# Two-product sums left in PSUM, raw words loaded earlier, and early row sums spread over query tiles, in a three-layer kernel

## The chip, the cores and the metric

The kernel runs on one core of one Trainium2 chip. The metric is the device time of one execution in microseconds (us). The notation of the profile: PE is TensorE, PEld its weight loads, DVE is VectorE, ACT is ScalarE, POOL is GpSimd and SP is the engine that issues most DMAs.

## The reference, cut to what matters

```python
# attention with keys and values averaged over groups of 8 positions
k_p = k.reshape(B, H, Sp, 8, D).mean(axis=3); v_p = v.reshape(B, H, Sp, 8, D).mean(axis=3)
scores = scale * q @ k_p.T ; attn = softmax(scores) ; x = attn @ v_p        # B=4, H=8, S=576, D=64
# layer 1: mixture of experts, all experts on all tokens, N=2304, D=512, E=8, F=1024
P = exp(x @ w_gate - max); eight times: P /= rows' sums, P /= columns' sums, P *= N / E
out = sum over e of P[:, e] * (maximum(x @ w1[e], 0) @ w2[e])
# layer 2: gated, F2=1536, its weights given as 64-bit floats
g = out @ w_gate2; silu = g / (1 + exp(-g)); result = (silu * (out @ w_val)) @ w_out
```

All arithmetic is to be accurate to fp32. Each fp32 operand of a matmul is split into a rounded half and a low part, and a product takes three matmuls (half times half, half times low part, low part times half).

## The kernel before

**Tiling.** The 2304 tokens are worked in three passes of TB = 768, each as two halves of HB = 384. The matrices of the experts are cut into 30 "quads" (a quad is 256 columns of w1 and the 256 rows of w2 that go with them; the first half of expert 0 is done apart, in the attention phase). Each quad's first product is a 2x2 block product done with seven products M1 to M7 in place of eight. Operands are the blocks B11, B21, B22 and the differences T1 to T4 of the token matrix. Each product is six matmuls of 128x384. Four results come out of them: "11" = M1 + M2, "21" (M1 + M6 + M7 + M4, all accumulated in one PSUM bank), "22" and "12". Three of the four are two-product sums: a bank of PSUM plus a partial sum that ScalarE had copied to SBUF (`part_sum`, line 1016: s1, u2, u3).

**PSUM.** Bank `a` has two buffers and holds the running sum M1, M6, M7, M4. Bank `b` has one and holds M2. Bank `c` holds M5, then M3 on top of it; it has two buffers in pass 0 and in the gated layer, one in passes 1 and 2.

**Stages.** (1) Attention, with the first half of expert 0 as filler for TensorE (`ready`, `fill`, `group0_units`); the loop runs over 20 query tiles. At the end of each tile, early_row_sums does four steps of the row sums of w2's blocks on GpSimd (line 187), their rounding on ScalarE (line 204), their low part on GpSimd (line 208), a store; these are later operands of the second product. (2) Pass 0, `quad`: seven products, then the second product tile by tile (`second_tile`, matmuls of 128x512 at lines 1086 to 1088), its result scaled by the routing weight and added in SBUF by VectorE (line 1328). From quad NEARLY on, row sums are made in this pass on VectorE (`row_sums`, line 187). (3) Passes 1 and 2, `expert_quad`, quads in pairs (q = 0, 1): the seven products of the first layer, weighting by the routing weight before the second product, and that one again in seven-product form (`block`, 12 matmuls of 128x384, accumulated into AC by VectorE at line 1270). The pairs number 30; the blocks of a pair are placed among the products of the next. A pair is 168 matmuls. (4) A tail of seven blocks, then the gated layer, 18 times a gate quad and a value quad (`gate_sink`, `value_sink`).

**Order.** All engines run the instructions in the order in which the program writes them; nothing is rescheduled. `late` is a queue of instructions that are issued at the next point between products (`later`). `side` is a queue of small steps, one of which is taken ("popped") at each point between products and after each block: 10 pops in the first quad of a pair, 11 in the second. The routing's iterations go through it in pass 0, the conversion of the gated layer's 64-bit weights in passes 1 and 2. For the conversion (`conv64`, `conv_steps`), a half block of raw words is loaded into one of two buffers of 512 KB, ScalarE takes the magnitude (line 934), VectorE does four more operations on 128x512 words and a fifth (line 951) that frees the buffer, GpSimd adds the two parts. Two halves make a block, 36 halves in all. All of these loads, as those of the experts' sets, go through the one SP queue, which waits in order.

**Around the weighting in passes 1 and 2.** `csum` writes a two-product sum to SBUF (line 1382), `weigh` takes the maximum with 0 times the routing weight (line 1390), in SBUF except for "21"; "22" and "12" are weighted in one 128x768 operation. `split_h` makes the rounded half on ScalarE (line 1227) and the low part on VectorE or GpSimd (line 1228); `sum_t13` and `sum_t24` (lines 1235, 1239) make the differences for the second product on GpSimd. The points at which they are issued are listed by hand with `on(q, point, ...)`, where a point is a product's name or the number of a block of the pair.

**Routing weights.** `load_pb` loads the weights of one expert and one pass, the same row for all 128 partitions; in the buffer in HBM a row lies in pieces of 128 floats.

## Time and profile before

| what | value |
|---|---|
| runs of the kernel | 2148.04, 2145.79, 2142.83 us; median 2145.79 |
| profiled execution | 2147.0 us; span of the core 2145.3 |
| TensorE busy | 2020.7 us, 94% of the span |
| VectorE, ScalarE, GpSimd busy | 1599.8 (75%), 806.2 (38%), 1323.7 (62%) |
[...]
| attention | to about 276 us |
| pass 0 | 276.5 to 766.9 us |
| passes 1 and 2 | 766.9 to 1716.9 us |
| gated layer | 1716.9 to 2145.3 us |

The stages are told by the first matmul on B11 of each quad. Matmuls overlap in the pipeline, so the busy time of TensorE hides short waits; the time per matmul in a stretch tells more. [...]

### The profile page before, as it was taken

The numbers are of one execution on the slowest core, as the hardware profiler recorded it, in microseconds if no ns is written. First come the engines' busy times: TensorE is split into PE (matmuls) and PEld (weight loads), VectorE is DVE, ScalarE is ACT, GpSimd is POOL, SyncE is SP. The second block draws the span as 40 slices with busy tenths as digits, with TensorE's granted clock in tenths as the row PEclk, the third lists the DMA queues.
The fourth block names the chain that finished last, engine by engine and source line by source line (L and its number), as shares of the span: only waits on it lengthen the run. The fifth ranks groups of instructions, "written<-read, shape, count | busy, mean of one in ns | idle before, by whom it ended". The sixth has DMA issues, their size and how long they took to land.

```text
span 2145.3 us, 30456 instructions
## 1 busy us (share of the span) xinstructions
PE 2020.7 (94%) x11079; PEld 1903.8 (89%) x11079; DVE 1599.8 (75%) x2119; ACT 806.2 (38%) x1461; POOL 1323.7 (62%) x1005
## 2 busy tenths in 40 slices
PE   7778789999999999999999999999999989999999
PEld 6677778888888889999999989998999889899898
DVE  7554366778778778997888888987655767767776
ACT  3333333444444442232322332332232354544543
POOL 4544556678788835767777656776655556445442
PEclk9989999999999999999999999999999999999999
DMA  6455457678888888888988888888888655453442
GB/s 175 138 150 142 123 201 253 224 281 298 289 284 304 291 276 310 307 293 306 310 299 315 276 285 310 298 315 300 267 261 258 211 191 166 168 193 131 163 140 96
DMA packets 227925, 514.82 MB, mean 240 GB/s; under 512 B 35424, under 2 KB 120000, under 8 KB 221632
## 3 DMA queue, kind: packets, MB, share of 16 engines
q1 hardware_dynamic: 222880, 497.15, 68.0%
q0 software_dynamic: 4896, 15.73, 2.6%
q8 instruction: 88, 1.44, 0.3%
q14 instruction: 61, 0.50, 0.1%
HBM read 361.78 MB, written 151.04 MB: 239 GB/s over the span
## 4 chain that ended last, share of the span: by engine, by line
PE 52%; DVE 22%; DMA 10%; issue 6%; POOL 5%; ACT 3%; SPq 1%; POOLq 0%; ACTq 0%; DVEq 0%
PE aps L114 5%; PE aps L116 5%; PE aps L115 5%; PE yps L1086 4%; PE yps L1088 4%; PE yps L1087 4%; PE mbs L114 4%; PE mbs L115 3%; PE mbs L116 3%; PE cps L114 3%; PE cps L116 2%; PE cps L115 2%; DVE LF L1390 2%; DVE LF L187 2%; DVE AC L1270 2%
## 5 line engine op out<-in xcount | busy, mean ns | idle before, releaser
L1016 ACT COPY LF<-aps 128x384 f32<-128x384 f32 x378 | 179.6, 475 | 536.8 <-PE aps L116 536.7
L114 PE MATMUL mbs<-LR 128*128 128x384 f32 x840 | 288.1, 343 | 10.0 <-DVE AC L1270 5.1
L115 PE MATMUL mbs<-LR 128*128 128x384 f32 x840 | 285.8, 340 | 1.0 <-DVE LR L1228 1.0
L116 PE MATMUL mbs<-LR 128*128 128x384 f32 x840 | 284.7, 339 | 0.0
L1228 POOL TENSOR_TENSOR LR<-LF,LR 128x768 fp32r<-128x768 f32 (+1 forms) x148 | 243.5, 1666 | 60.1 <-ACT LR L1227 56.7
L1227 ACT ACTIVATE LR<-LF 128x768 fp32r<-128x768 f32 (+1 forms) x240 | 174.7, 761 | 208.1 <-DVE LF L1390 180.1
L1270 DVE TENSOR_TENSOR AC<-mbs,AC 128x768 f32<-128x768 f32 x196 | 185.9, 950 | 75.4 <-PE mbs L116 74.8
L1086 PE MATMUL yps<-LR 128*128 128x512 f32 x576 | 228.5, 397 | 12.1 <-DVE AC L1328 11.7
L1088 PE MATMUL yps<-LR 128*128 128x512 f32 x576 | 225.6, 392 | 0.5 <-DVE LR L1532 0.5
L1087 PE MATMUL yps<-LR 128*128 128x512 f32 x576 | 225.4, 391 | 0.0
L770 POOL TENSOR_TENSOR LR<-praw,LR 128x512 fp32r<-128x512 f32 (+1 forms) x130 | 135.2, 1060 | 140.9 <-ACT LR L764 140.9
L1239 POOL TENSOR_TENSOR LF<-LF 128x384 f32<-128x384 f32 x120 | 154.1, 1284 | 95.3 <-DVE LR L1228 90.6
L770 POOL TENSOR_TENSOR LR<-sums,LR 128x1024 fp32r<-128x1024 f32 x65 | 160.0, 2462 | 53.5 <-ACT LR L764 53.4
L1235 POOL TENSOR_TENSOR LF<-LF 128x768 f32<-128x768 f32 x60 | 117.2, 1954 | 122.5 <-DVE LF L1390 122.4
L114 PEld LDWEIGHTS mbs<-LR 128*128 128x128 f32 x840 | 160.3, 191 | 14.3 <-DVE AC L1270 8.9
L115 PEld LDWEIGHTS mbs<-LR 128*128 128x128 f32 x840 | 160.6, 191 | 1.3 <-DVE LR L1228 1.3
L116 PEld LDWEIGHTS mbs<-LR 128*128 128x128 f32 x840 | 160.2, 191 | 0.0
L66 POOL TENSOR_TENSOR LR<-rraw,LR 128x512 fp32r<-128x512 f32 x72 | 112.9, 1590 | 68.6 <-ACT LR L65 58.1
L1086 PEld LDWEIGHTS yps<-LR 128*128 128x128 f32 x576 | 108.5, 188 | 37.8 <-DVE AC L1328 18.6
L1390 DVE SCALAR_TENSOR_TENSOR LF<-LF,LR 128x384 f32<-128x384 f32 x120 | 138.4, 1154 | 4.1
L1328 DVE SCALAR_TENSOR_TENSOR AC<-yps,pr,AC 128x512 f32<-128x512 f32 x168 | 121.0, 742 | 25.3 <-PE yps L1088 25.2
L1088 PEld LDWEIGHTS yps<-LR 128*128 128x128 f32 x576 | 108.5, 188 | 24.5 <-DVE LR L1532 1.0
(289 smaller groups left out, 5750.1 us busy)
## 6 DMA issues: line engine op xcount, KB each, us to landing
LR<-w1s_d SPq DMA_DIRECT2D x210, 512.0 KB, 5.8
LR<-w2s_d SPq DMA_DIRECT2D x210, 512.0 KB, 5.6
w1s_d<-LR SPq DMA_DIRECT2D x29, 1792.0 KB, 8.5
w2s_d<-LR SPq DMA_DIRECT2D x90, 256.0 KB, 5.7
w2s_d<-LR SPq DMA_DIRECT2D x22, 1024.0 KB, 4.2
praw<-in_moe_w_dram SPq DMA_DIRECT2D x30, 512.0 KB, 5.2
rraw<-in_moe_w_dram SPq DMA_DIRECT2D x30, 512.0 KB, 4.5
LR<-rows_d POOLq DMA_DIRECT2D x12, 1024.0 KB, 7.1
```

The source lines that it names most:

```text
L114: nc.tensor.matmul(ps, lhsT=wh, rhs=ah, start=start, stop=False, skip_group_check=more)
L115: nc.tensor.matmul(ps, lhsT=wh, rhs=al, start=False, stop=False, skip_group_check=more)
L116: nc.tensor.matmul(ps, lhsT=wl, rhs=ah, start=False, stop=stop, skip_group_check=more)
L770: nc.gpsimd.tensor_tensor(out=lo, in0=src, in1=hi.bitcast(F32), op=ALU.subtract)
L1016: nc.scalar.copy(out=t, in_=ps[:, :HB])
L1086: nc.tensor.matmul(ps, lhsT=hh[:, o:o + P], rhs=wh, start=j == 0, stop=False)
L1087: nc.tensor.matmul(ps, lhsT=hh[:, o:o + P], rhs=wl, start=False, stop=False)
L1088: nc.tensor.matmul(ps, lhsT=hl[:, o:o + P], rhs=wh, start=False, stop=j == 1)
L1227: nc.scalar.activation(out=hi, in_=src, func=AF.Copy)
L1228: f = lambda: eng.tensor_tensor(out=lo, in0=src, in1=hi.bitcast(F32), op=ALU.subtract)
L1270: nc.vector.tensor_tensor(out=acc_of(m), in0=ps[:, :, :HB], in1=acc_of(m), op=ALU.add)
L1390: nc.vector.scalar_tensor_tensor(out=r, in0=r if src is None else src[:, :HB], scalar=0.0, in1=w, op0=ALU.max, op1=ALU.mult)
```

## The change

- Early row sums: 7 instead of 8. One step per query tile instead of four: the four sums in one tile; in the next the rounding, the low parts and the next load; the store one tile later still.
- Routing weights are laid out in HBM so that one expert's row of a pass is contiguous (768 floats); the one store becomes 12.
- Conversion: the load of a half stands 7 pops ahead of its first use (before 4) and two pops behind the fifth step (before one); a half takes 14 pops (before 11), the stores stand later.
- `whole`: a two-product sum is written back into its bank of PSUM; "22", whose bank `c` is needed for M3, goes to a new buffer of bank `b`. All users read it from there: in pass 0 and the gated layer ScalarE and VectorE, in passes 1 and 2 the weighting, which for "11", "22" and "21" writes to PSUM again.
- `split_b`, for "11", "22" and "21": ScalarE copies the weighted value to SBUF (for GpSimd's differences) and rounds it, VectorE takes the low part from PSUM. "12" goes to SBUF only. `split_t`, for the differences, has both low parts on GpSimd.
- The points of `split_b`, `split_t` and the differences move.
- The transposed result of pass 0 (`transposed`) goes to the free half of AC instead of a two-deep buffer.

```diff
-    P_d = dram.tile([NT - TT, E, P], F32, name="P_d")
+    P_d = dram.tile([E, N - TB], F32, name="P_d")
-    NEARLY = 8
+    NEARLY = 7
...
-        for i in range(NEARLY):
+        def load(i):
             r = rawp.tile([P, 2, DM], F32, tag="raw", name=f"early{i}")
             nc.sync.dma_start(out=r, in_=rows[i].rearrange("(j p) d -> p j d", p=P))
+            return r
+
+        r = load(0)
+        for i in range(NEARLY):
             yield
+            if i > 0:
+                keep_row_sums(i - 1, w)
             for f in take_row_sums(nc.gpsimd, r, t):
                 f()
-                yield
+            yield
             nc.scalar.activation(out=w[:, :, 0], in_=t, func=AF.Copy)
-            yield
             for c in range(2):
...
-                yield
-            keep_row_sums(i, w)
+            if i + 1 < NEARLY:
+                r = load(i + 1)
+        yield
+        keep_row_sums(NEARLY - 1, w)
...
-                for _ in range(4):
-                    next(early_sums, None)
+                next(early_sums, None)
...
-            side.append(lambda: nc.sync.dma_start(out=P_d.rearrange("t e c -> (t e) c"), in_=pt[:n, 0:P]))
+            def store():
+                for t in range(NT - TT):
+                    nc.sync.dma_start(out=P_d[:, t * P:(t + 1) * P], in_=pt[t * E:(t + 1) * E, 0:P])
+            side.append(store)
...
-            yield from [loads[0], n, n, n]
-            stored = n
+            yield from [loads[0]] + [n] * 6
             for i, (halves, begin, out_sums, store) in enumerate(pairs):
                 for j, (_, c) in enumerate(halves):
-                    yield from [c[0], stored, c[1], c[2], begin if j == 0 else n, c[3], c[4], loads[2 * i + j + 1],
-                                n, out_sums if j == 1 else n, n]
-                    stored = store if j == 1 else n
-            yield from [n, stored]
+                    yield from [c[0], c[1], c[2], n if j else begin, c[3], c[4], n, loads[2 * i + j + 1],
+                                out_sums if j else n, n, n, n, store if j else n, n]
...
+        def whole(name, ps, t):
+            if t is None:
+                return ps[:, :HB]
+            out = (new_b() if name == "22" else ps)[:, :HB]
+            nc.vector.tensor_tensor(out=out, in0=ps[:, :HB], in1=t, op=ALU.add)
+            return out
...
-                src = ps[:, :HB]
-                if t is not None:
-                    src = part_of(TEMP[name], HB, F32)
-                    nc.vector.tensor_tensor(out=src, in0=ps[:, :HB], in1=t, op=ALU.add)
+                src = whole(name, ps, t)
...
-            x2 = part_of(16.5 + 2 * (t % 2), DM, F32).rearrange("p (k t) -> p k t", k=KD)
+            x2 = acc_view(TT + t).rearrange("p (k t) -> p k t", k=KD)
...
-                src = P_d[(p - 1) * TT:p * TT, e, :]
-                nc.sync.dma_start(out=pb_of(p * E + e).rearrange("p (t c) -> p t c", t=TT),
-                                  in_=src.partition_broadcast(P))
+                nc.sync.dma_start(out=pb_of(p * E + e), in_=P_d[e, (p - 1) * TB:p * TB].partition_broadcast(P))
...
+        def split_b(q, m, name):
+            src = weighed.pop((q, name))
+            hi, lo = h_of(q, m)
+            nc.scalar.copy(out=r_of(q, name), in_=src)
+            nc.scalar.activation(out=hi, in_=src, func=AF.Copy)
+            late.append(lambda: nc.vector.tensor_tensor(out=lo, in0=src, in1=hi.bitcast(F32), op=ALU.subtract))
...
+        def split_t(q, m, name, eng):
+            hi, lo = (h_pair(q, m, 2)[:, :, h] for h in (0, 1))
+            src = r_of(q, name, 2)
             nc.scalar.activation(out=hi, in_=src, func=AF.Copy)
             f = lambda: eng.tensor_tensor(out=lo, in0=src, in1=hi.bitcast(F32), op=ALU.subtract)
...
-            def csum(name, ps, t):
-                nc.vector.tensor_tensor(out=r_of(q, name), in0=ps[:, :HB], in1=t, op=ALU.add)
-
-            def weigh(name, n, src=None):
-                r = r_of(q, name, n)
+            def weigh(name, ps, t):
+                src = whole(name, ps, t)
                 h = int(name[1]) - 1
-                w = pb[:, h * HB:(h + 1) * HB]
-                if n > 1:
-                    w = w.unsqueeze(1).to_broadcast([P, n, HB])
-                nc.vector.scalar_tensor_tensor(out=r, in0=r if src is None else src[:, :HB], scalar=0.0, in1=w,
+                if name == "12":
+                    out = r_of(q, name)
+                else:
+                    out = weighed[q, name] = src
+                nc.vector.scalar_tensor_tensor(out=out, in0=src, scalar=0.0, in1=pb[:, h * HB:(h + 1) * HB],
                                                op0=ALU.max, op1=ALU.mult)
...
-            point("M2", lambda: csum("11", banks["b"], s1), lambda: weigh("11", 1))
+            point("M2", lambda: weigh("11", banks["b"], s1))
...
-            point("M7", lambda: csum("22", banks["c"], u3))
+            point("M7", lambda: weigh("22", banks["c"], u3))
...
-            point("M4", lambda: weigh("21", 1, banks["a"]))
+            point("M4", lambda: weigh("21", banks["a"], None))
...
-            point("M3", lambda: csum("12", banks["c"], u2), lambda: weigh("12", 2))
+            point("M3", lambda: weigh("12", banks["c"], u2))
...
-            on(0, 1, lambda: split_h(0, "M1", "11", 1, G))
-            on(0, "M3", lambda: sum_t13(0))
-            on(1, 3, lambda: split_h(0, "M3", "22", 2, V))
-            on(1, "M6", lambda: sum_t24(0))
-            on(1, 4, lambda: split_h(0, "M5", "11", 2, G), lambda: split_h(1, "M1", "11", 1, G))
-            on(1, "M3", lambda: sum_t13(1))
-            on(1, 6, lambda: split_h(1, "M3", "22", 2, V), lambda: split_h(0, "M6", "22", 2, V))
+            on(0, 0, lambda: split_b(0, "M1", "11"))
+            on(0, 2, lambda: split_b(0, "M3", "22"))
+            on(0, "M3", lambda: split_b(0, "M2", "21"))
+            on(1, "M1", lambda: sum_t13(0), lambda: sum_t24(0))
+            on(1, 3, lambda: split_b(1, "M1", "11"))
+            on(1, 4, lambda: split_t(0, "M5", "11", G))
+            on(1, 5, lambda: split_b(1, "M3", "22"))
+            on(1, "M3", lambda: split_b(1, "M2", "21"))
+            on(1, 6, lambda: split_t(0, "M6", "22", G), lambda: sum_t13(1), lambda: sum_t24(1))
...
-            on(0, "M2", lambda: sum_t24(1))
-            on(0, 1, lambda last=last: split_h(1, "M5", "11", 2, V if last else G))
-            on(0, 2, lambda last=last: split_h(1, "M6", "22", 2, V if last else G))
+            on(0, 1, lambda last=last: split_t(1, "M5", "11", V if last else G))
+            on(0, 2, lambda last=last: split_t(1, "M6", "22", V if last else G))
...
-                nc.vector.tensor_tensor(out=g, in0=src, in1=g, op=ALU.mult)
+                src = whole(name, ps, t)
+                nc.vector.tensor_tensor(out=src, in0=src, in1=g, op=ALU.mult)
```

## Rows read from the trace of the kernel before

**Rows 1.** Busy time of each engine in seven stretches (columns as in the second line).
```profile
core 0: us, PE busy (x) PEld busy (x) DVE busy (x) ACT busy (x) POOL busy (x), PEclk, DMA share, GB/s
85.00:241.00 156.00, 118.97 (x801) 109.00 (x800) 64.77 (x113) 50.86 (x101) 74.25 (x88) 0.88 0.60 161
375.70:406.70 31.00, 31.00 (x158) 28.12 (x157) 22.44 (x29) 12.27 (x24) 21.53 (x18) 1.00 0.65 235
406.70:442.90 36.20, 33.16 (x158) 29.16 (x157) 28.43 (x37) 13.73 (x26) 25.32 (x19) 0.95 0.68 244
459.10:751.20 292.10, 283.93 (x1407) 252.24 (x1406) 230.76 (x307) 127.49 (x235) 240.71 (x180) 1.00 0.83 292
813.50:1504.10 690.60, 664.46 (x3699) 653.53 (x3698) 600.73 (x703) 211.35 (x350) 476.34 (x325) 0.98 0.86 301
1504.10:1665.90 161.80, 161.80 (x931) 161.80 (x930) 99.25 (x122) 46.22 (x77) 90.71 (x63) 1.00 0.83 264
1716.90:2145.30 428.40, 415.72 (x2162) 384.86 (x2160) 308.17 (x436) 207.07 (x401) 199.25 (x137) 1.00 0.46 156
```

**Rows 2.** Waits of TensorE, 85 to 241 us: us in total, times, longest.
```profile
PE hps L114 <- ACT qT L307: 20.7, 4, 7.1
PE gps L404 <- ACT lt L397: 7.2, 1, 7.2
```

**Rows 3.** Waits of ScalarE in the same stretch.
```profile
ACT AC L204 <- POOL AC L187: 49.3, 7, 9.6
```

**Rows 4.** Waits of GpSimd in the same stretch.
```profile
POOL x_d L514 <- PE mps L315: 23.8, 3, 9.9
```

**Rows 5.** Waits of TensorE, 766.9 to 1716.9 us.
```profile
PE aps L114 <- ACT LF L1016: 18.0, 12, 3.0
PE mbs L114 <- DVE AC L1270: 5.1, 7, 2.2
PE cps L114 <- DVE LF L1382: 5.0, 8, 1.6
PE mbs L114 <- ACT LF L1164: 4.4, 1, 4.4
```

**Rows 6.** Waits of ScalarE, 780 to 1500 us.
```profile
ACT LF L934 <- DMA craw<-in_moe_w_val_dram: 41.4, 12, 10.3
ACT LF L934 <- DMA craw<-in_moe_w_gate_dram: 39.7, 11, 5.2
ACT LF L934 <- DMA craw<-in_moe_w_out_dram: 38.9, 10, 9.6
```

**Rows 7.** SP's issues in order of time, 974 to 993 us.
```profile
979.02 0.38 SPq L928 DMA_DIRECT2D craw<-in_moe_w_val_dram  x1
```

**Rows 8.** ScalarE in order of time, 974 to 996 us: start, length, instruction, idle before.
```profile
987.94 0.66 ACT L934 ACTIVATE LF<-craw 128x512 f32<-128x512 f32 x1 [10.31 <-DMA craw<-in_moe_w_val_dram]
```

**Rows 9.** DMA issues: count, KB each, median us to landing.
```profile
LR<-P_d SPq DMA_DIRECT2D x16, 384.0 KB, 9.8
```

**Rows 10.** VectorE's groups by shape, 780 to 1504 us: busy us, mean ns, idle before.
```profile
L1228 DVE TENSOR_TENSOR LR<-LF,LR 128x768 fp32r<-128x768 f32 x69 | 77.2, 1145 | 7.6 <-ACT LR L1227 7.5
L1390 DVE SCALAR_TENSOR_TENSOR LF<-LF,LR 128x768 f32<-128x768 f32 x46 | 57.9, 1259 | 1.6
L1390 DVE SCALAR_TENSOR_TENSOR LF<-LF,LR 128x384 f32<-128x384 f32 x46 | 53.8, 1169 | 1.6
...
L1390 DVE SCALAR_TENSOR_TENSOR LF<-aps,LR 128x384 f32<-128x384 f32 x47 | 25.7, 547 | 1.5 <-PE aps L116 0.8
```

**Rows 11.** A group of ScalarE by shape, whole span.
```profile
L1227 ACT ACTIVATE LR<-LF 128x384 fp32r<-128x384 f32 x60 | 30.7, 512 | 5.7 <-DVE LF L1390 5.7
```

**Rows 12.** VectorE in order of time in a quad of pass 0.
```profile
512.35 0.56 DVE L1107 SCALAR_TENSOR_TENSOR LR<-LF,LR 128x384 fp32r<-128x384 f32 x1 [0.59 <-ACT LR L1106]
```

**Rows 13.** VectorE in order of time in a clean pair.
```profile
1528.27 0.96 DVE L1270 TENSOR_TENSOR AC<-mbs,AC 128x768 f32<-128x768 f32 x1 [3.05 <-PE mbs L116]
1529.88 0.56 DVE L1382 TENSOR_TENSOR LF<-cps,LF 128x384 f32<-128x384 f32 x1 [0.65 <-ACT LF L1016]
```

**Rows 14.** TensorE in order of time in the same pair.
```profile
1534.33 0.34 PE L114 MATMUL bps<-B21h,LR 128*128 128x384 f32 x1
```

More of the change, by code (lines that the diff above doesn't have):

```diff
@@ L1010, in product @@
                     start and k == 0, k == 1, not start)
-        TEMP = {"s1": 0, "u2": 1.5, "u3": 3, "11": 4.5, "22": 6, "12": 7.5}
+        TEMP = {"s1": 0, "u2": 1.5, "u3": 3}
         def part_sum(ps, name):
@@ L1220, in fused_kernel @@
         GT = AC[:, 7 * TB:8 * TB].rearrange("p (c t) -> p c t", c=2)
-        def split_h(q, m, name, n, eng):
-            hi, lo = (h_pair(q, m, n)[:, :, h] for h in (0, 1))
-            src = r_of(q, name, n)
-            if n == 1:
-                hi, lo = hi[:, 0], lo[:, 0]
+        def split_t(q, m, name, eng):
+            hi, lo = (h_pair(q, m, 2)[:, :, h] for h in (0, 1))
+            src = r_of(q, name, 2)
             nc.scalar.activation(out=hi, in_=src, func=AF.Copy)
@@ L1232, in split_h @@
                 f()
+        weighed = {}
+        def split_b(q, m, name):
[4 more added lines that the diff above has]
+            late.append(lambda: nc.vector.tensor_tensor(out=lo, in0=src, in1=hi.bitcast(F32), op=ALU.subtract))
         def sum_t13(q):
@@ L1439, in fused_kernel @@
                 tr = [lambda t=t: transposed(t) for t in range(TT)]
[L1440 to L1441 removed]
+                fills = {0: ys[0:2], 1: ys[2:3], 2: ys[3:4], 3: ys[4:6], 4: tr[0:2], 5: tr[2:4], 6: tr[4:6]}
             last = j == NPR - 1
[L1443 to L1449 removed]
+            on(0, 0, lambda: split_b(0, "M1", "11"))
[7 more added lines that the diff above has]
+            on(1, 6, lambda: split_t(0, "M6", "22", G), lambda: sum_t13(1), lambda: sum_t24(1))
             expert_quad(j, 0, fills)
@@ L1468, in fused_kernel @@
             later()
-            for k in {0: ((0, "M2"), (0, 1)), 2: ((0, 2),)}.get(a, ()):
+            for k in {0: ((0, 1),), 2: ((0, 2),)}.get(a, ()):
                 for f in do.pop(k):
@@ L1502, in sink @@
                 g = gp_of(("11", "22", "21", "12").index(name))
-                src = ps[:, :HB]
-                if t is not None:
-                    nc.vector.tensor_tensor(out=g, in0=src, in1=t, op=ALU.add)
-                    src = g
+                src = whole(name, ps, t)
                 sg = gp_of(4 + next(turn) % 2)
@@ L1522, in sink @@
                 g = gs[name]
-                src = ps[:, :HB]
-                if t is not None:
-                    src = gp_of(6 + next(turn) % 2)
-                    nc.vector.tensor_tensor(out=src, in0=ps[:, :HB], in1=t, op=ALU.add)
-                nc.vector.tensor_tensor(out=g, in0=src, in1=g, op=ALU.mult)
+                src = whole(name, ps, t)
+                nc.vector.tensor_tensor(out=src, in0=src, in1=g, op=ALU.mult)
                 hh, hl = h_tiles(hs, name, n)
                 def parts():
-                    nc.scalar.activation(out=hh, in_=g, func=AF.Copy)
-                    late.append(lambda: nc.vector.tensor_tensor(out=hl, in0=g, in1=hh.bitcast(F32), op=ALU.subtract))
+                    nc.scalar.activation(out=hh, in_=src, func=AF.Copy)
+                    late.append(lambda: nc.vector.tensor_tensor(out=hl, in0=src, in1=hh.bitcast(F32), op=ALU.subtract))
                 late.append(parts)
```

2 lines of the change are left out of this document (removed).

## The prediction

> **What bounds the kernel now.** I read the busy shares by stage first, then the waits of TensorE stage by stage, then, for each wait, the queue of the engine that was waited for. The stages differ, so each is judged by its own pace [rows 1]. The last stage (the gated layer) runs 2162 matmuls in 428.4 us with the clock at 1.00, and the early quads of pass 0 (375.7 to 406.7, 15.50 us each) have TensorE busy all of the time: there TensorE is the bound and nothing is to be had. The same is true of passes 1 and 2 from 1504.1 to 1665.9, where no conversion of the 64-bit weights is left in the side queue: 931 matmuls in 161.8 us, 0.1738 us each. Two stretches are different.
>
> [...] TensorE waits 20.7 + 7.2 = 27.9 us for ScalarE's copies there, in five waits [rows 2]. ScalarE in turn waits 49.3 us, in seven times of up to 9.6 us, for one thing: line 204 (the rounded half of the early row sums) behind GpSimd's sums at line 187 [rows 3]. ScalarE works in order, so the copies of queries and of attention weights queue behind line 204, and the matmuls behind them. That is a wait on a by-product, not on attention.
>
> Passes 1 and 2 with conversions (813.5 to 1504.1): 3699 matmuls in 690.6 us. At the pace of the clean stretch they take 3699 x 0.1738 = 642.9, so 47.7 us are lost, some of it waits and some the clock (0.98). TensorE's waits of the whole two passes name line 1016 (ScalarE's copy of a partial sum) with 18.0 us, VectorE's sums with 5.0 and 5.1, and line 1164 with 4.4 [rows 5]. ScalarE's own largest foreign wait is for the raw 64-bit words: 41.4 + 39.7 + 38.9 = 120 us in 33 waits [rows 6]. One of them shows the chain: the load is issued at 979.02, after the queue on SP had waited for VectorE's fifth step; the words are there at 987.94, after 10.31 us in which ScalarE did nothing, partial sums included [rows 7, 8].
>
> **The change part by part.**
>
> *Early row sums: 7 and not 8, one step per query tile.* Removed: ScalarE no longer reaches line 204 before GpSimd has the sums, since those are issued one tile earlier; the load is issued one tile before the sums, and the store waits on SP one tile later. What could go is 27.9 us of waits [rows 2] and the clock's loss of at most 0.12 x 156 = 18.7 us [rows 1], 47 us together. It can't all go. GpSimd, also in order, has 74 us of work in this stretch [rows 1] and waits another 23.8 us, in three waits, at line 514, where a store of attention's output must land before the second half is added to it [rows 4]; the change leaves these. So no less than 98 of the 156 us, and its other waits come on top. I take 28 us, all of the waits or most of them and some of the clock, between 12 (a second wait stands close behind most of the first ones) and 45.
>
> The eighth sum goes to pass 0, quad 7: four VectorE additions at line 187 ahead of the accumulations of y. Quads that have them take 292.1 / 18 = 16.23 us against 15.50 without, and quads 8 and 9, which have a difference of token operands on VectorE too, 36.2 together [rows 1]. Quad 7 is of that kind: +1.5 us, bounds +0.7 (16.23 - 15.50) and +3.7 (36.2 less 16.23 and less 16.23).
>
> *Raw words 7 pops ahead.* A pair of quads has 21 pops; at 690.6 us for 22 pairs a pop is 1.5 us. From the fifth step (which frees the buffer) to the next use there were 5 pops, now 9: 6 us more. The mean wait was 120 / 33 = 3.6 us [rows 6]; the long ones of up to 10.3 us follow a load of routing weights. Steps per half grow from 11 to 14, so the conversions spread from about quad 47 to quad 57 of the 60, still before the tail (402 steps become 511; I counted the pops off quad by quad). The number of conversions stays, and each costs VectorE and ScalarE the same, only thinner.
>
> *Routing weights contiguous.* The 16 loads of 384 KB took a median of 9.8 us [rows 9]; they now come as 3 KB rows in place of 512-byte pieces. It matters through the words' load queued behind: that of rows 7 and 8 took 8.9 us. The 12 small stores in place of one lie on SP in pass 0, where nothing waits: 0.
>
> *Two-product sums, weights and low parts in PSUM.* In the conversion stretch a weighting of 128x384 with both operands in SBUF takes 1169 ns, one of 128x768 1259, one of 384 from PSUM 547; the low part of 768 takes 1145 [rows 10]. Per pair of quads: two weightings of each SBUF kind become six of 0.547 (4.86 to 3.28), three low parts of 768 become six of 384 (3.44 to 3.28 at 0.547 each). VectorE saves 1.7 us of about 31 per pair. No row of before has VectorE write to PSUM; I take 0.55 us for it, as for its reads. Bounds: nothing saved, or twice the price, which puts VectorE 6 us a pair up and is the rival below. ScalarE gets twelve copies of 384, at 0.512 [rows 11], and gives up two of that form and two wider ones: at most 5.1 us a pair more, on an engine with 211 / 22 = 9.6 of 31.4 us busy [rows 1]. I cost that at nothing, since only its partial sums are waited for; if each of the six in a pair came 0.5 us later than TensorE can bear, it would be 3 us a pair.
>
> Why the SBUF form is slow bears on this. The same 384-wide operation, in SBUF alone, took 0.56 us at its quickest [rows 12]: as fast as from PSUM. So the 1169 is not the memory's own pace but something that holds the operation up, and that is expected to be gone with an operand in PSUM. [...]
>
> *Transposes' result in the accumulator's free half.* Removes the 4.4 us wait at line 1164, ScalarE behind a store out of a two-deep buffer [rows 5].
>
> Of the two passes, then, 47.7 + 4.4 = 52.1 us are open. Half of VectorE's 5.0 + 5.1 [rows 5] I leave standing, and 5 us for a word load that is still late and for the bank below: 42 gained, bounds 20 and 52.
>
> **Sum.** -28 + 1.5 - 42 = -68.5. The profiled execution took 2147.0 us (span 2145.3), 1.2 above the median of the runs; 2147.0 - 68.5 = 2078.5, and I put 2078.
>
> **Rivals.**
>
> *The words are late for another reason (SP's order), so the waits stay.* For it: the load of rows 7 was issued late, not only landed late. Against: the lead grows behind the step that held SP up. Then the two passes give 10, in all -28 + 1.5 - 10: 2110. Chance 0.13.
>
> *Attention's next wait stands right behind.* GpSimd's waits at line 514 [rows 4] speak for it; that ScalarE's idle time at line 204 is longer than all that TensorE loses [rows 2, 3], against. It gives 10 in place of 28: 2096. Chance 0.16.
>
> *Slower: the one bank b is handed back late.* It takes the sum of M1 + M2, is kept until the low part is taken, then the second two-product sum, kept again; M2 of the next quad must wait for that. In a clean pair the sum of 22 starts at 1529.88 [rows 13]; with it and its weighting (0.56 each), two copies on ScalarE (0.51 each [rows 11]), an accumulation of 768 in between (0.96 [rows 13]) and the low part (0.55) it is free at 1533.5 at the latest, and M2 of the next quad starts at 1534.33 [rows 14]: 0.8 us to spare. The kernel becomes slower only if this costs more than the 68.5 gained, 2.3 us in each of 30 pairs, that is, if the chain is 3.1 us longer than this. VectorE's operations at twice the price (three of them, +1.7) don't reach that: 0.9 x 30 = 27 us. If two more operations of 0.96 stood in the chain every time, conversions for the most part, it would be (1.7 + 1.9 - 0.8) x 30 = 84 and the kernel at 2078.5 + 84 = 2162. Chance 0.05. [...]
>
> *It does little:* both gains fail, -10 + 1.5 - 10: 2128. Chance 0.04.
>
> **How the numbers follow.** My forecast has 0.62. Its own range: gains of 45 + 52 - 0.7 to about 18 + 30 - 3.7, so 2051 to 2103. To leave out no more than 2 in 10 the upper end must take in the two rivals at 2096 and 2110, with a margin for the mixed cases: 2050 to 2116. A measurement of this kernel tells 0.2% (4.3 us) from no change. Faster by more than that: 0.62 + 0.13 + 0.16 + 0.04 less a little for what no case names, 0.93; within it 0.03; slower 0.04.
>
> **What would show it.** ScalarE's wait at line 204 gone and the clock above 0.95 in attention; ScalarE's waits for raw words under 30 us in all; pairs of quads with conversions near 29.4 us, not 31.4; weightings near 0.55 us whatever GpSimd does; line 1164 without wait. Wrong if M2 (bank b) shows up among TensorE's waits with more than 10 us, if an operation of VectorE into PSUM takes 0.8 us or more, if attention's stretch is still over 145 us, or if conversions run on into the tail after the last quad.

## The result and the profile after

The changed kernel took 2050.19 us (median of 4 runs, 2047.7 to 2051.81); the kernel before, beside it, 2145.15 (median of 4). The ratio is 0.9556, 95% interval 0.9539 to 0.9572. The forecast was 2078: the kernel gained 28 us more than that, and the time stands at the very edge of the range (2050 to 2116); the profiled execution, 2047.7, lies below it. By stages, each told by the first matmul on B11 of a quad, profile against profile:

| stage | before | after | difference | forecast |
|---|---|---|---|---|
| attention | 276.5 | 238.8 | -37.7 | -28 |
| pass 0 | 490.4 | 472.3 | -18.1 | +1.5 |
| passes 1 and 2 | 950.0 | 908.7 | -41.3 | -42 |
| gated layer | 428.4 | 426.2 | -2.2 | 0 |
| span | 2145.3 | 2046.0 | -99.3 | -68.5 |

These are one profile of each kernel. How far a stage differs between executions can be seen in the runs below that leave it alone. Attention and pass 0 hold to a few us: 274.5 to 277.9 and 488.7 to 490.6 as before, 236.1 to 238.8 and 472.0 to 472.4 as changed. Passes 1 and 2 do not: 939.6 to 946.6 in four runs that have them as in the kernel before (950.0 there), and 908.0 to 915.9 in eight that have them as changed. With these two profiles the means are 944.3 and 911.0, which is 33 us apart. So the 41.3 us of that stage may be high by several us, and differences of a few us in it tell nothing.

The page of the changed kernel, its span and the engines' shares of the chain that ended last:

```profile
span 2046.0 us, 30950 instructions
...
PE 84%; DVE 10%; ACT 2%; DMA 2%; issue 1%; POOL 1%; SPq 0%; DVEq 0%; ACTq 0%; POOLq 0%
```

The busy times in the stretches that answer to [rows 1] (columns as there). The stretch of attention has the same 156 us and ends as long before pass 0, but does not hold the same work; the others begin within 1 us of the same quad, the 18 quads of pass 0 one quad earlier:

```profile
47.30:203.30 156.00, 142.42 (x1028) 129.20 (x1027) 98.08 (x156) 66.25 (x133) 91.99 (x116) 0.98 0.65 177
338.00:369.00 31.00, 30.80 (x155) 27.58 (x154) 22.32 (x32) 12.95 (x25) 21.53 (x18) 1.00 0.63 223
368.60:401.10 32.50, 31.52 (x158) 28.01 (x157) 26.39 (x37) 14.18 (x27) 26.82 (x20) 1.00 0.81 282
401.10:680.10 279.00, 279.00 (x1406) 253.04 (x1406) 205.49 (x307) 125.74 (x235) 229.84 (x180) 1.00 0.86 306
...
750.80:1408.20 657.40, 649.12 (x3698) 643.79 (x3698) 544.65 (x775) 264.60 (x519) 410.50 (x288) 1.00 0.88 305
...
1408.20:1570.00 161.80, 161.80 (x931) 161.80 (x930) 124.01 (x190) 66.08 (x130) 101.00 (x71) 1.00 0.89 309
1619.80:2046.00 426.20, 415.32 (x2161) 385.42 (x2160) 257.92 (x436) 205.92 (x401) 195.78 (x137) 1.00 0.46 157
```

In 156 us of attention TensorE now runs 1028 matmuls, where it ran 801, at a granted clock of 0.98 and not 0.88. Eighteen quads of pass 0 with row sums take 279.0 us, 15.50 each, where they took 292.1: the pace that only quads without row sums had. The 22 pairs that had the conversions went from 690.6 to 657.4 us. About half of this is waiting and half is TensorE's own pace: its busy time for the same matmuls fell from 664.5 to 649.1 us (granted clock 0.98, then 1.00), its idle time from 26.1 to 8.3. The last stretch of 161.8 us is as long as before, though it now holds conversions too.

The waits of TensorE and ScalarE in attention that answer to [rows 2, 3] (us in total, times, longest):

```profile
PE hps L114 <- ACT qT L314: 4.2, 2, 3.8
...
PE gps L411 <- ACT lt L404: 0.5, 1, 0.5
...
ACT AC L210 <- POOL AC L187: 6.8, 2, 4.6
...
ACT AC L210 <- DMA w2s_d<-AC: 4.5, 1, 4.5
```

And the waits of TensorE in passes 1 and 2, beside [rows 5]:

```profile
PE mbs L114 <- DVE AC L1287: 3.5, 3, 2.5
PE aps L114 <- ACT LF L1024: 3.5, 3, 1.9
PE cps L114 <- DVE bps L1109: 2.6, 3, 1.8
PE bps L114 <- DVE LR L1249: 1.7, 2, 1.2
```

Of TensorE's 27.9 us of waits [rows 2] 4.7 are left. ScalarE at line 210 (204 before) waits 6.8 us for the sums, not 49.3, and 4.5 us, once, for the store of the sums before. TensorE's wait for the partial sum fell from 18.0 to 3.5; ScalarE no longer waits for raw words at all, where it waited 120 us [rows 6]. Bank `b`, the rival that would have made the kernel slower, is there with 1.7 us. The wait at line 1164 is gone. VectorE's groups by shape in the changed kernel, 757 to 1466 us, beside [rows 10] (busy us, mean ns, idle before):

```profile
L1405 DVE SCALAR_TENSOR_TENSOR bps<-bps,LR 128x384 f32<-128x384 f32 x95 | 53.8, 567 | 3.3
L1249 DVE TENSOR_TENSOR LR<-bps,LR 128x384 fp32r<-128x384 f32 x95 | 52.2, 550 | 1.9
...
L1109 DVE TENSOR_TENSOR cps<-cps,LF 128x384 f32<-128x384 f32 x47 | 26.4, 561 | 2.6 <-PE cps L116 1.8
...
L1405 DVE SCALAR_TENSOR_TENSOR LF<-cps,LR 128x384 f32<-128x384 f32 x47 | 26.2, 558 | 4.0
```

On average VectorE's operations here that write to PSUM take 0.56 to 0.57 us, and those that write to SBUF from there 0.55 and 0.56: the price that was assumed for want of a row.

### The profile page after: what moved, and what is told of

Read it like the earlier page. It is cut to its first block, busy times and chain, and to the rows that moved or that the text cites. A ratio compares the mean times of both kernels' runs of the same rounds, so it can differ in the third digit from the quotient of the medians.

```text
span 2046.0 us, 30950 instructions
## 1 busy us (share of the span) xinstructions
PE 1986.9 (97%) x11079; PEld 1884.8 (92%) x11079; DVE 1485.6 (73%) x2273; ACT 880.9 (43%) x1701; POOL 1243.9 (61%) x970
## 4 chain that ended last, share of the span: by engine, by line
PE 84%; DVE 10%; ACT 2%; DMA 2%; issue 1%; POOL 1%; SPq 0%; DVEq 0%; ACTq 0%; POOLq 0%
PE aps L114 8%; PE aps L116 8%; PE aps L115 8%; PE mbs L114 6%; PE mbs L115 6%; PE mbs L116 6%; PE yps L1094 6%; PE yps L1096 6%; PE yps L1095 6%; PE cps L114 4%; PE cps L116 4%; PE cps L115 4%; PE bps L114 2%; PE bps L116 2%; PE bps L115 2%
## 5 line engine op out<-in xcount | busy, mean ns | idle before, releaser
L1236 POOL TENSOR_TENSOR LR<-LF,LR 128x768 fp32r<-128x768 f32 x118 | 221.2, 1878 | 192.8 <-ACT LR L1235 192.8
L1247 ACT COPY LF<-bps 128x384 f32<-128x384 f32 x120 | 57.8, 481 | 244.1 <-DVE bps L1405 244.1
L114 PEld LDWEIGHTS mbs<-LR 128*128 128x128 f32 x840 | 158.5, 189 | 4.5 <-DVE AC L1287 4.5
L115 PEld LDWEIGHTS mbs<-LR 128*128 128x128 f32 x840 | 158.5, 189 | 0.0
L116 PEld LDWEIGHTS mbs<-LR 128*128 128x128 f32 x840 | 158.4, 189 | 0.0
L66 POOL TENSOR_TENSOR LR<-rraw,LR 128x512 fp32r<-128x512 f32 x72 | 100.8, 1420 | 58.5 <-ACT LR L65 48.6
L1256 POOL TENSOR_TENSOR LF<-LF 128x384 f32<-128x384 f32 x120 | 130.2, 1085 | 9.4
L1109 DVE TENSOR_TENSOR bps<-cps,LF 128x384 f32<-128x384 f32 x126 | 70.9, 563 | 78.6 <-ACT LF L1024 78.2
```

Source lines behind the costliest of these rows:

```text
L114: nc.tensor.matmul(ps, lhsT=wh, rhs=ah, start=start, stop=False, skip_group_check=more)
L115: nc.tensor.matmul(ps, lhsT=wh, rhs=al, start=False, stop=False, skip_group_check=more)
L116: nc.tensor.matmul(ps, lhsT=wl, rhs=ah, start=False, stop=stop, skip_group_check=more)
L1236: f = lambda: eng.tensor_tensor(out=lo, in0=src, in1=hi.bitcast(F32), op=ALU.subtract)
L1256: nc.gpsimd.tensor_tensor(out=r_of(q, a), in0=r_of(q, a), in1=r_of(q, b), op=ALU.subtract)
```

## Where pass 0's 18 us come from

This is the stage that I had down for +1.5. A quad of pass 0 in each kernel: it begins at 507.8 before (quad 14) and at 509.6 after (quad 17). It need not be the same one, since the quads 10 to 27 are alike: 16.21 to 16.25 us before, 15.50 after. VectorE in order of time before, the rows around [rows 12] (start, length, instruction, idle before):

```profile
510.02 1.27 DVE L1107 SCALAR_TENSOR_TENSOR LR<-LF,LR 128x384 fp32r<-128x384 f32 x1 [1.47 <-ACT LR L1106]
511.22 0.54 DVE L1102 TENSOR_TENSOR LF<-bps,LF 128x384 f32<-128x384 f32 x1
...
512.83 1.52 DVE L187 TENSOR_TENSOR LF<-rraw 128x256 f32<-128x256 f32 x1
...
516.91 2.06 DVE L1328 SCALAR_TENSOR_TENSOR AC<-yps,pr,AC 128x512 f32<-128x512 f32 x3
```

GpSimd in the same quad of the kernel before:

```profile
508.47 2.41 POOL L66 TENSOR_TENSOR LR<-LF,LR 128x1024 fp32r<-128x1024 f32 x1 [2.75 <-ACT LR L65]
510.84 3.23 POOL L66 TENSOR_TENSOR LR<-rraw,LR 128x512 fp32r<-128x512 f32 x2
```

And TensorE, the first matmul that waits for the result, with its neighbours:

```profile
516.91 0.34 PE L116 MATMUL aps<-T3h,LR 128*128 128x384 f32 x1
517.70 0.50 PE L1086 MATMUL yps<-LR 128*128 128x512 f32 x1 [0.45 <-DVE AC L1328]
518.04 0.40 PE L1087 MATMUL yps<-LR 128*128 128x512 f32 x1
```

TensorE's only waits in the 18 quads, 442.9 to 734.9 us (us in total, times, longest):

```profile
PE yps L1086 <- DVE AC L1328: 8.2, 18, 0.5
```

These lines show a chain. The low part of "12", two operands in SBUF, is issued at 510.02, while GpSimd works on 128x1024 until 510.88; it ends at 511.29, 0.41 us after that. The first row sum, both operands in SBUF, ends at 514.35, 0.28 after GpSimd's pair that ended at 514.07. So VectorE begins the accumulations of y 9.1 us after the quad's start, and TensorE, whose three banks of y are full, idles 0.45 us, once in each of the 18 quads. That is more than 0.45 us lost: the waiting matmul starts 0.79 us after the one before it, where 0.17 is the pace of those, and the next one 0.34 after it, where 0.23 is. Together that is 0.73, which is what every such quad takes longer (16.22 less 15.50). VectorE in the changed kernel, in order of time:

```profile
511.78 0.56 DVE L1119 SCALAR_TENSOR_TENSOR LR<-cps,LR 128x384 fp32r<-128x384 f32 x1 [1.43 <-ACT LR L1118]
512.26 0.56 DVE L1109 TENSOR_TENSOR bps<-bps,LF 128x384 f32<-128x384 f32 x1
513.37 0.56 DVE L1119 SCALAR_TENSOR_TENSOR LR<-bps,LR 128x384 fp32r<-128x384 f32 x1 [0.56 <-ACT LR L1118]
513.85 0.41 DVE L187 TENSOR_TENSOR LF<-rraw 128x256 f32<-128x256 f32 x1
514.29 1.41 DVE L187 TENSOR_TENSOR LF<-LF,rraw 128x256 f32<-128x256 f32 x1
...
517.38 2.06 DVE L1345 SCALAR_TENSOR_TENSOR AC<-yps,pr,AC 128x512 f32<-128x512 f32 x3
```

And GpSimd beside it:

```profile
510.26 2.41 POOL L66 TENSOR_TENSOR LR<-LF,LR 128x1024 fp32r<-128x1024 f32 x1 [2.65 <-DMA w2s_d<-LR]
512.63 2.79 POOL L66 TENSOR_TENSOR LR<-rraw,LR 128x512 fp32r<-128x512 f32 x2
```

The low part has one operand in PSUM and takes 0.56 us under the same operation of GpSimd. GpSimd's pair of 128x512 takes 2.79 us and not 3.23. The row sums start 4.25 us after the quad's start (5.03 before) and end 7.9 after it (9.2 before); TensorE has no such wait left. Of the 18.1 us of the stage, 13.0 come from these 18 quads and 0.9 from the two behind them, 3.7 from quads 8 and 9 (36.2, now 32.5) and 0.9 from quads 0 to 6; quad 7 takes 0.5 back. I read this as a hold-up by GpSimd of VectorE's operations with both inputs in SBUF: the ends 0.41 and 0.28 us behind GpSimd's agree, and so does the 0.56 with one input in PSUM. By what means the one engine holds up the other is not shown.

## The experiments

Each run stands beside the kernel before, and its ratio to that is given with its 95% interval. Stage times are from one profile of each run.

### Parts of the change, one at a time

**The early row sums alone** (before, with the new generator and one step per query tile).

```diff
-    NEARLY = 8
+    NEARLY = 7
...
-                for _ in range(4):
-                    next(early_sums, None)
+                next(early_sums, None)
```

> The kernel before, with the early row sums of the change alone (7 in place of 8, one step per query tile). Theory: attention's stretch falls by all that it fell in the change, 36 to 38 us, and pass 0 grows by 1 to 4 us for the eighth row sum, so the kernel is 33 to 37 us faster, about 2110. Rival (GpSimd's contiguous routing store or the other parts share in it): attention falls by less than 25.

2102.86 us, ratio 0.9800 (0.9782 to 0.9818): a few us more gained than the 33 to 37 expected. Attention takes 237.4 us (-39.1), ScalarE's wait for the sums is 6.7 us, and the clock is 0.98 in the same stretch. All of attention's gain is this part's. Pass 0 stays at 491.1, its quad 7 rises from 15.50 to 17.00 (+1.5, as forecast for the eighth sum).

**The conversion's lead alone.**

```diff
-            yield from [loads[0], n, n, n]
+            yield from [loads[0]] + [n] * 6
...
-                    yield from [c[0], stored, c[1], c[2], begin if j == 0 else n, c[3], c[4], loads[2 * i + j + 1],
-                                n, out_sums if j == 1 else n, n]
+                    yield from [c[0], c[1], c[2], n if j else begin, c[3], c[4], n, loads[2 * i + j + 1],
+                                out_sums if j else n, n, n, n, store if j else n, n]
...
```

> The kernel before, with the conversion's loads 7 pops ahead and its steps spread to 14 a half, nothing else. Theory (the lead does it): passes 1 and 2 take 25 to 35 us less than 950, ScalarE's waits for raw words fall from 120 to under 30 us, the kernel is near 2115. Rival (VectorE, slowed by GpSimd, is what makes TensorE late, or the routing loads make the words late whatever the lead): passes 1 and 2 gain 10 us or less.

2113.55 us, ratio 0.9851 (0.9836 to 0.9866); passes 1 and 2 in 916.2 us (-33.8). ScalarE's waits for raw words in this kernel:

```profile
ACT LF L934 <- DMA craw<-in_moe_w_val_dram: 2.1, 2, 1.9
ACT LF L934 <- DMA craw<-in_moe_w_gate_dram: 1.3, 1, 1.3
```

That is 3.4 us of 120. The rival that SP's order would keep the words late falls with this run.

**The contiguous routing weights alone** (with the 12 small stores that go with them).

```diff
-    P_d = dram.tile([NT - TT, E, P], F32, name="P_d")
+    P_d = dram.tile([E, N - TB], F32, name="P_d")
...
+                nc.sync.dma_start(out=pb_of(p * E + e), in_=P_d[e, (p - 1) * TB:p * TB].partition_broadcast(P))
```

> The kernel before, with the routing weights' rows contiguous in HBM, nothing else. Theory: the long waits for raw words, which follow a routing load, shrink, since that load lands in about 6.4 us and not 9.8; passes 1 and 2 gain 5 to 12 us. Rival (the words are late for lack of lead alone): under 3 us.

2121.64 us, ratio 0.9895 (0.9879 to 0.9911), 22.5 us less; passes 1 and 2 in 923.4 us (-26.6), where 5 to 12 us were expected. ScalarE's waits for raw words here:

```profile
ACT LF L940 <- DMA craw<-in_moe_w_out_dram: 35.1, 11, 7.6
ACT LF L940 <- DMA craw<-in_moe_w_gate_dram: 33.9, 11, 6.0
ACT LF L940 <- DMA craw<-in_moe_w_val_dram: 28.7, 11, 6.5
```

97.7 us of the 120 remain, and yet more than half of the gain of these passes is there. The longest waits went (7.6 us at most, not 10.3), and TensorE's wait for the partial sum fell from 18.0 to 10.3. That the long waits are what counts is argued, not shown: the run of the PSUM form below cuts them further and gains less. The total idle time of an engine off the path, at any rate, said little.

**Both of these.**

> The kernel before with both parts that make the raw words early, the lead of 7 pops and the contiguous routing rows, and nothing else. Alone they took 34 and 27 us from passes 1 and 2, together more than the 52 that were open there. If both remove the same waits, the two together gain 36 to 42 us and PSUM's part is worth at most 5 in the whole change; if they remove different ones, they gain 48 or more and PSUM's part costs time in these passes.

2109.51 us, ratio 0.9852 (0.9813 to 0.9891); passes 1 and 2 in 909.6 us (-40.4). The two gains, 33.8 and 26.6 by the stage and 1.5% and 1.05% by the runs, don't add up: they remove the same waits. By the runs the two together are not told apart from the lead alone (0.9851).

**The PSUM form in passes 1 and 2 and the gated layer alone** (pass 0 as before; the diff of `weigh`, `split_b` and `split_t`).

```diff
-            def csum(name, ps, t):
-                nc.vector.tensor_tensor(out=r_of(q, name), in0=ps[:, :HB], in1=t, op=ALU.add)
...
+                src = whole(name, ps, t)
...
```

> The kernel before, with the PSUM form and the new points of split_b and split_t in passes 1 and 2 and the gated layer alone; early row sums, conversion, routing layout, transposes and pass 0 as before. Theory (the words' waits are what costs; VectorE's relief is small beside them): passes 1 and 2 gain 3 to 15 us of 950. Rival (VectorE's lateness is at the root of the late words): 25 us or more. Second rival (bank b's wait): passes 1 and 2 get longer, and TensorE's waits name bps.

2136.03 us, ratio 0.9967 (0.9956 to 0.9979): 7 us less. Passes 1 and 2 take 939.5 us (-10.5), a difference within what this stage scatters. Three of TensorE's waits there:

```profile
PE aps L114 <- ACT LF L1015: 10.6, 7, 2.4
PE bps L114 <- DVE LR L1245: 8.1, 8, 1.9
PE cps L114 <- DVE bps L1100: 5.5, 4, 2.9
```

The second is the forecast's rival in the open: M2 waits for bank `b` behind the low part, 8 times, where conversions are still held up by their words. With the words early it is 1.7 us. So bank `b` is tight, but it doesn't turn the sign. ScalarE's waits for words fell in this run too, from 120 to 52.6 us with 6.1 as the longest, and TensorE's wait for the partial sum to 10.6; the waits for banks `b` and `c` took most of that back.

### Pass 0: which sum, and why

**"12" alone in PSUM** (the three runs of this kind differ in the names listed).

```diff
-                    src = part_of(TEMP[name], HB, F32)
+                    if name not in ('12',):
+                        src = part_of(TEMP[name], HB, F32)
+                    elif name == "22":
+                        src = new_b()[:, :HB]
```

> The kernel before, with one thing of the change: in pass 0 the two-product sum 12 stays in PSUM (its rounding and low part read it there); 11 and 22 go to SBUF as before. In the profile of before the low part of 12 took 1.27 us beside a GpSimd operation, and the sum of 11, ScalarE's rounding of it, its low part and the row sums stand behind it in order; in the profile of after that low part took 0.56 and the quads fell from 16.22 to 15.50 us. Theory one (that low part alone starts the chain that TensorE waits for): quads 10 to 28 of pass 0 take 15.5 to 15.6 us, the kernel 13 to 18 us less, about 2130. Rival (all three sums matter, or the row sums themselves are freed): quads stay above 16.0, the kernel within 4 us of before.

2131.18 us, ratio 0.9942 (0.9922 to 0.9963); pass 0 481.1 us, quads 10 to 27 at 15.87: half of the gain. The low part of "11" in this kernel, VectorE in order of time:

```profile
507.51 0.95 DVE L1110 SCALAR_TENSOR_TENSOR LR<-LF,LR 128x384 fp32r<-128x384 f32 x1 [0.59 <-ACT LR L1109]
```

"12" no longer waits, but everything behind it comes earlier, and "11", which slipped through in 0.56 before [rows 12], is now held up for 0.95.

**"11" and "22" in PSUM, "12" not.**

```diff
+                    if name not in ('11', '22'):
```

> The kernel before, with 11 and 22 of pass 0 in PSUM and 12 in SBUF as before: the complement of the run with 12 alone, in which quads 10 to 28 took 15.87 us (before 16.22, after 15.50), since the hold-up by GpSimd had moved from the low part of 12 to that of 11 (0.95 us). Chain theory (the low part of 12 comes first in order, so while it is held up the rest has nothing to give): quads at 16.1 to 16.25. Rival (the parts add up, each its share): 15.85.

2130.99 us, ratio 0.9933 (0.9912 to 0.9953); pass 0 478.6 us, quads at 15.87. A miss: I expected that without "12" next to nothing would be had, and half was. The low part of "12" is held up as ever:

```profile
517.69 1.27 DVE L1110 SCALAR_TENSOR_TENSOR LR<-LF,LR 128x384 fp32r<-128x384 f32 x1 [1.47 <-ACT LR L1109]
```

What is gained comes behind it: GpSimd's pair ends 5.91 us after the quad's start (6.27 before, 5.83 after), and the row sums, which start when they did, end 0.35 us earlier.

**"11" and "12", not "22".**

```diff
+                    if name not in ('11', '12'):
```

> The kernel before, with 11 and 12 of pass 0 in PSUM and 22 in SBUF. 12 alone gave quads of 15.87 us and 11 with 22 gave 15.87, out of 16.22. If two low parts, of 12 and of 11, stand one after the other in the chain to the row sums, the two together give 15.50 and pass 0 is 470 to 473 us; if 22 carries a share, the quads stay at 15.6 or above.

2127.02 us, ratio 0.9922 (0.9896 to 0.9949); pass 0 471.9 us, quads at 15.50: all of it. "22" has no share.

**The changed kernel with pass 0's sums back in SBUF.**

```diff
...
-                src = whole(name, ps, t)
+                src = ps[:, :HB]
+                if t is not None:
+                    src = part_of(TEMP[name], HB, F32)
+                    nc.vector.tensor_tensor(out=src, in0=ps[:, :HB], in1=t, op=ALU.add)
```

> The kernel after, with pass 0's three two-product sums back in SBUF. Chain theory: pass 0 returns to about 490 us and quads 10 to 28 to 16.2, the kernel is 16 to 20 us slower than after, near 2068; no other stage moves by more than 3 us. Rival (the early row sums or the other parts gave pass 0 its gain): pass 0 stays within 5 us of 472.

2070.87 us, ratio 0.9659 (0.9644 to 0.9673), 20.7 above the changed kernel's 2050.19; pass 0 491.1 us, quads at 16.23. Passes 1 and 2, where nothing was edited, have 913.2, 4.5 more, which is within this stage's scatter. The form of the sums and nothing else is pass 0's gain; the runs of the other parts leave the stage at 488.7 to 491.1.

**Out of GpSimd's way instead** (before, with the split of the row sums, GpSimd's line 66, moved to the next quad).

```diff
-                        at("M2", lambda: store_row_sums(n - 1))
+                        at("M2", lambda: split_row_sums(n - 1), lambda: store_row_sums(n - 1))
...
-                        at("M4", lambda: split_row_sums(n))
...
```

> The kernel before, all sums in SBUF, with one thing moved: in pass 0 the rounding and low part of the row sums (the GpSimd operation of 2.4 us that the low part of 12 collides with) are issued two products later. If it is GpSimd's overlap that holds the low part of 12 up, and not SBUF as such, that low part takes 0.56 us and quads 10 to 28 lie near 15.87 or below, unless the moved operation now collides with the row sums behind it. If SBUF as such is slow, its 1.27 stays and the quads at 16.2.

2218.1 us, ratio 1.0347 (1.0326 to 1.0368). VectorE in a quad of pass 0, in order of time:

```profile
568.25 0.56 DVE L1107 SCALAR_TENSOR_TENSOR LR<-LF,LR 128x384 fp32r<-128x384 f32 x1 [1.47 <-ACT LR L1106]
...
570.65 1.13 DVE L1107 SCALAR_TENSOR_TENSOR LR<-LF,LR 128x384 fp32r<-128x384 f32 x1 [1.37 <-ACT LR L1106]
574.08 0.94 DVE L187 TENSOR_TENSOR LF<-rraw 128x256 f32<-128x256 f32 x1 [2.29 <-POOL LR L66]
```

GpSimd in the same stretch:

```profile
568.81 2.55 POOL L66 TENSOR_TENSOR LR<-rraw,LR 128x512 fp32r<-128x512 f32 x2 [7.25 <-ACT LR L65]
571.32 2.72 POOL L66 TENSOR_TENSOR LR<-LF,LR 128x1024 fp32r<-128x1024 f32 x1
```

On the disputed point the run is clean: the low part of "12", in SBUF, takes 0.56 us where GpSimd is idle, and that of "11", which meets GpSimd, 1.13, its end 0.42 after GpSimd's (571.36). As a kernel it fails for another reason: the next row sum now waits 2.29 us until GpSimd has read the old ones out of the buffer.

### What is left in attention

**One early sum instead of seven** (changed kernel).

```diff
-    NEARLY = 7
+    NEARLY = 1
```

> The kernel after with one early row sum in place of 7; the others are made in pass 0. It asks how much of attention's stretch the early sums still hold up. If GpSimd's order is attention's floor, as the prediction had it, the stretch falls by another 8 us or more; if TensorE and its next waits are, by less than 4. In pass 0 quads 1 to 6 get row sums: at most 1.5 us each where VectorE has other work, 0 to 9 us in all.

2049.49 us, ratio 0.9572 (0.9533 to 0.9611): no difference. Attention falls to 221.6 us (-17.2), clock 1.00 between 30 and 186 us; pass 0 rises by 13.7 to 486.0. Passes 1 and 2 have 915.9 (+7.2) with no edit there, the longest of the runs that have them as changed. The sums still cost attention 17 us when spread out, and pass 0 nearly as much when it has them. By the expectation, 8 us or more meant that GpSimd's order is attention's floor; but the run takes the sums' work from ScalarE and the DMA queue too, so it shows that the sums still bind, not through which engine.

**Eight sums, from one tile earlier**, twice.

```diff
-    NEARLY = 7
+    NEARLY = 8
...
-            if i > 3:
+            if i > 2:
```

> The kernel after with 8 early row sums, one step per query tile from one tile earlier on. If it is the spreading over tiles that freed attention, its stretch stays within 4 us of 238.8 and quad 7 of pass 0 returns to 15.50; if the eighth sum was what was too much, attention takes 5 us more.

2040.56 us, ratio 0.9530 (0.9489 to 0.9571, two runs), attention 230.0.

> The kernel after with 8 early row sums from one tile earlier, again and in more rounds: attention at 230 us, pass 0 at 471.5, the kernel 8 to 11 us faster than after, near 2040. If the first look was chance, it is within 3 us of after.

2047.05 us, ratio 0.9538 (0.9508 to 0.9569), attention 235.4. The first run's gain did not hold. In its profile TensorE had 94 matmuls in the first 20 us, in the second 76: attention's start differs by some microseconds from one execution to another. For this one kernel the faster start (granted clock 1.00 in those 20 us, against 0.83) went with 5.4 us less attention.

**Seven sums, from one tile earlier**, twice, with the changed kernel beside it.

```diff
-            if i > 3:
+            if i > 2:
```

> The kernel after, with its 7 early row sums started one query tile earlier. With 8 from one tile earlier attention fell to 230.0 us from 238.8. If the tile on which the heavier step falls (rounding, low parts and next load) is what counts, 7 from one tile earlier give 228 to 232 as well; if the start is not what counts, 237 to 240.

> The kernel after, unchanged, beside the version with 8 early sums on the same chip: 2045 to 2052.

2038.85 us, ratio 0.9510 (0.9468 to 0.9552, two runs), beside 2043.96, 0.9536 (0.9507 to 0.9565), for the changed kernel: not told apart.

> The changed kernel with the seven early sums issued one query tile earlier still, once more, beside the changed kernel. If its first time (2038.85 us) was real: 2036 to 2041 us, attention 225 to 232 us, ratio to the kernel before 0.950 to 0.952. If it was the scatter of attention's start, as with the eight sums: 2044 to 2051 us, attention 232 to 239 us, within 0.2% of the changed kernel beside it.

> The changed kernel itself, on the same chip: 2043 to 2051 us, attention 236 to 240 us.

2037.9 us, ratio 0.9517 (0.9502 to 0.9532), beside 2047.34, 0.9563 (0.9544 to 0.9581). The intervals are apart: with the earlier sums the kernel is 0.5% faster than the changed kernel beside it. From the eight sums (0.9508 to 0.9569) it is not told apart. Attention from 20 us on with the earlier sums (columns as in [rows 1]):

```profile
20.00:225.80 205.80, 190.32 (x1409) 174.67 (x1410) 137.07 (x224) 90.77 (x180) 126.33 (x140) 0.98 0.61 164
```

And in the changed kernel beside it:

```profile
20.00:237.20 217.20, 195.17 (x1414) 178.55 (x1414) 139.45 (x227) 90.64 (x180) 129.55 (x142) 0.97 0.57 156
```

Nearly the same work takes 205.8 and 217.2 us. Passes 1 and 2 have 912.6 for 908.9, within their scatter. Why attention gains is open: ScalarE's wait for the sums did not fall (8.6 us, 6.7 beside it), and no single wait of TensorE accounts for 11 us. Chance may have a share: both profiles with seven earlier sums had the fast start (94 matmuls in 20 us at a clock of 1.00), and none of the changed kernel's had it (78 to 89 at 0.83 to 0.91).

### The boundary between passes

**The additions of VectorE at a pass's end, through the side queue** (changed kernel).

```diff
-                for f in combine(1 + j // (NQ // 2), m):
-                    late.append(f)
+                side.extend(combine(1 + j // (NQ // 2), m))
```

> The kernel after; at the end of pass 1 the additions that combine the blocks go into the side queue, one per pop, in place of five in a row. There VectorE works 4.8 us on them in one piece, and TensorE waits for bank b and for partial sums in the four quads around it, which take 11 us more than clean ones. Theory: these quads lose 3 to 6 us, the kernel is about 2046. Rival: the low parts of the token operands just ahead of them are what costs, and nothing is gained (within 2 us).

2045.75 us, ratio 0.9547 (0.9521 to 0.9573): not told apart from the changed kernel. The boundary's quad fell from 18.76 to 14.91 us, and from there to the end of the passes the quads took 4.1 us less in all, within the 3 to 6 expected. Passes 1 and 2 stayed at 909.1 (908.7) because two quads at the beginning of pass 1, ahead of the edit, took 4.4 us more. In another profile of the unchanged version the boundary's quad took 17.19, so part of the fall may be scatter; whether the edit is worth anything is open.

## Why the prediction was right and wrong

**Pass 0 (+1.5): the step that failed.** The term was put as "Quad 7 is of that kind: +1.5 us, bounds +0.7" and +3.7. It costed the eighth sum's quad and left the other quads alone: their 16.23 us were read as what row sums cost, and used as a price. They were 15.50 plus a stall that the change removes. Measured, the term is -18.1 us. Three rows could have said so: the low part at 1.27 us, GpSimd's operation across it, and TensorE's wait for VectorE at line 1086, 18 times 0.45; [rows 1] itself has TensorE idle for 8.2 of the 292.1 us. I had the rule for passes 1 and 2, from the quick 0.56 of [rows 12], a row of pass 0, and did not apply it where that row comes from. Quad 7 in itself went as said in the run of the early sums alone (+1.5), and with the PSUM form it is +0.5 (15.99). With -18.1 in this term's place the sum is 2147.0 - 28 - 18.1 - 42 = 2058.9.

**Attention (-28): mechanism right, size off.** ScalarE's wait at line 204 went and TensorE's waits behind it; measured -37.7, within the bounds of 12 and 45. The 27.9 us of waits came nearly whole (4.7 are left), and the clock seems to have given more than the "some of" it that I allowed. A matmul's busy time in the stretches of 156 us fell from 118.97 / 801 = 0.1485 to 142.42 / 1028 = 0.1385 us, 10 us over 1028 of them; that the clock is all of this is argued, not shown. What the trace of the kernel before shows of it: matmuls of 128x256 start 0.21 us apart where the granted clock is 0.50 (234.4 to 236.0 us), and 0.12 apart where it is 1.00 (238.1 to 239.3). The floor that I worked out from GpSimd's 98 us was not reached, but that the sums still bind was right: with one of them instead of seven attention loses another 17.2.

**Passes 1 and 2 (-42): right, -41.3 in the profile, the closeness partly luck.** With this stage's scatter the gain may as well be 33; that is still within the bounds of 20 and 52. Within the 41.3, the stretch with conversions gave 33.2, its beginning (766.9 to 813.5, now 711.1 to 750.8) 6.9 and the end 1.2. I argued it from the lead, with the routing weights as a help; alone, the lead gives 33.8, the routing weights 26.6 and the PSUM form 10.5 by the profiles (31.9, 22.5 and 7 by the runs' ratios), and what the last adds to the first two together, 0.9, is below what the profiles tell. The transposes' part was not run alone. VectorE's saving in passes 1 and 2 is real and hardly on the path. ScalarE's extra copies (264.6 us busy for 211.4 in the 22 pairs) cost nothing that shows, as said.

**The rivals.** SP's order: refuted by the lead alone. Attention's next wait: not there, -37.7. Bank `b`: 1.7 us, and 8.1 where the words are late; it never came near the 68.5 that it would have had to eat. That the change does little: each part but the PSUM form of passes 1 and 2 gives over 0.4% by itself.

## What to carry to other kernels

A slower group of quads is not a price until the trace says what its extra time is: look for the wait of the bounding engine in it before using it as a cost. When an edit frees an operation of a hold-up in one stage, apply it in every stage that has the same operation beside the same neighbour. And two cures for one wait are not added: what is open in a stage bounds their sum. A stage time from one profile is compared only when its scatter over unedited runs is known.

## What was not expected of the hardware

- In these traces the hold-up between VectorE (two inputs in SBUF) and GpSimd goes both ways and moves on: freed at "12" it met "11" (0.56 to 0.95 us), and GpSimd's own 128x512 pair went from 3.23 to 2.79 us when VectorE read PSUM.
- Only a step that ends late costs. Row sums that end 9.2 us after the quad's start cost 0.72 us a quad, 8.85 cost 0.37 ("12" alone, or "11" and "22"), 7.9 nothing.
- Sixteen loads of routing weights in pieces of 512 bytes, 9.8 us each [rows 9], cost the kernel some 22 us (ratio 0.9895 without them). In the traces the last packet of such a load ends 9.5 us (median) behind its issue, and 5.4 in the changed kernel, where the rows are contiguous. That they cost it by holding back the loads behind them is argued.
